# Two tiles of the first layer turned by VectorE instead of TensorE, the launch reordered, and a new order for everything else

## The chip, the cores and the metric

The kernel runs on one core of one Trainium2 chip. The metric is the device time of one execution, in microseconds (us); less is better. Before the change it is 876.21 us, the median of 3 runs (875.59 to 876.23).

TensorE (PE in the profile) multiplies a stationary 128x128 block with a moving block of up to 512 columns into a PSUM bank. VectorE (DVE) and ScalarE (ACT) read and write SBUF and PSUM, GpSimd (POOL) works in SBUF, and SyncE (SP) issues most of the DMAs. The program gives each engine its own list of instructions, and an instruction carries the waits for what it reads and overwrites.

## The reference: what is computed

Two layers over x of 2048 rows and 448 columns, in float32, each layer a linear attention block (A) and a dense block (B) with the same weights in both layers:

```
x = x + A(layernorm(x));  x = x + B(layernorm(x))       # twice
A: q, k, v = x @ wqkv in 16 heads of 28; phi(t) = (t + 1 if t > 0 else exp(t)) + 1e-6
   kv = sum over rows of phi(k) v;  z = sum over rows of phi(k)
   o = phi(q) kv / (phi(q) z + 1e-6);  A = o @ wo
B: gelu(x @ w1 + b1) @ w2 + b2                           # 448 -> 1792 -> 448
```

## The kernel before

The rows are cut into 16 tiles of 128 rows. To keep float32 accuracy, each operand is split into a rounded part (`hi`, type fp32r) and the rest (`lo`), and a product is made as hi*hi + hi*lo + lo*hi. That is why each product of a tile with a 448-column weight is a group of 11 matmuls of 448 columns.

In the attention stage of a layer each tile t is loaded (`ld`), its mean and variance are taken (`a`: three small VectorE instructions; the first tile's come first at the launch), GpSimd makes the reciprocal root (`ar`, tile `brs`), VectorE normalises it in place (`n`, the TENSOR_SCALAR x<-x,bmv,brs). The normalised tile has to be turned, columns onto partitions, before TensorE can multiply it. There are two ways:

- **by TensorE** (`T`, function `pe_turn`): ScalarE makes a doubled tail (`d`), four 128x128 transposes go into a PSUM bank `tp`, ScalarE casts the bank to the hi part `XH` (`xh`) and VectorE subtracts to get the lo part `XL` (`xl`, XL<-tp,XH).
- **in squares by VectorE** (`tu`, function `turn`): two STREAM_TRANSPOSE instructions turn 32x32 squares into the SBUF buffer `sq`, which two neighbouring tiles share; one DMA stores the pair to DRAM (`st`, sq_a<-sq), four DMAs read it back with the squares in their places (`sp`, sp<-sq_a), and `xh` and `xl` then read the SBUF buffer `sp` (XL<-sp,XH).

In layer 0, tiles 0 and 1 are turned by TensorE in halves at the launch (`ht`, `hx`, `hl`, `hk`), tiles 2 to 5 by `T`, tiles 6 to 15 in squares. In layer 1 all sixteen go in squares.

From the turned tile TensorE makes K (`K`, bank psk) and Q (`Q`, bank psq). phi of K goes ScalarE (`ke`), VectorE (`kp`), ScalarE (`kh`), VectorE (`kl`); VectorE adds phi(K) to a running sum (`za`). K has two PSUM banks, so tile t's K group can start only when `za` and `kl` of the K group two before it have read that bank. `G` adds up the normalised tile times phi(K) over the rows in four PSUM banks. After the sixteenth tile come the products with wv (`kv`, bank kvp), its masking to heads (`mask`), its hi part on ScalarE (`mkh`, kvh) and lo part on VectorE (`mkl`, kvl), and the products with wo (`m`). Then each tile's output (`o` for tiles 0 to 3, `oc` for the others), the second layernorm, and block B: `f` (11 matmuls of 512 columns), gelu (`g`), its split (`gh`, `gl`) and `y` (12 matmuls of 448 columns), for four groups of 14.

What sets the order is one string of tokens for each layer (`ORDER`), written out by a program that planned it beforehand. `run` calls each token's function in turn, and so each engine's list comes out in that order. `hot16` at the launch is 16 matmuls of 512 columns on a block of ones, which compute nothing. A token with > belongs to the next layer.

Of the kernel before, what the change touches and what calls it, by code (L numbers as in the profile page):

```python
# [118 lines left out]
def linear_attn_mlp_kernel(  # L119
# [84 lines left out]
    T = {}  # L204
# [141 lines left out]

    def stats(xs):
        st = small(6, "bst")  # L350
        dve.bn_stats(st, xs)  # L351
        mv = small(2, "bmv")
# [629 lines left out]
```

## Time and profile before

| what | before |
| --- | --- |
| median of 3 runs | 876.21 us (875.59 to 876.23) |
| the profiled execution's own time | 877.34 us |
| its span, first to last instruction | 875.6 us |
| TensorE busy | 870.3 us (99%), 4189 matmuls |
| VectorE busy | 477.5 us (55%) |
| ScalarE busy | 344.2 us (39%) |
| GpSimd busy | 208.7 us (24%) |
| granted TensorE clock | 1.0 |

Busy time of TensorE is the union of pipelined matmuls whose ends are modelled, so a short wait can hide in it. A row of the timeline holds start, length, engine, line, operation and tiles; waits of TensorE are best read from the starts of neighbouring rows. A line such as L365 is a line of the kernel before; in the changed kernel the same code stands 1 to 10 lines lower.

### The profile page before, as it was taken

What the parts mean: (1) busy time and instruction counts of PE and PEld (TensorE: products, weight loads), DVE (VectorE), ACT (ScalarE), POOL (GpSimd) and SP (SyncE); (2) the same over time, 40 slices, a digit from 0 to 9 for tenths busy, and PEclk for the clock granted to TensorE, in tenths of its full rate; (3) what the DMA queues carried; (4) which work ended last, traced back from release to release, by engine and by line L of the source; (5) the groups of instructions that cost most, each with busy time, mean ns of one, the idle gap of its engine ahead of it and who ended that gap; (6) DMA issues with size and microseconds to landing.
All of it is one profiled execution on the core that took longest, in us unless ns stands there. A gap on an engine that the chain in (4) does not pass through costs nothing.

```text
span 875.6 us, 11616 instructions
## 1 busy us (share of the span) xinstructions
PE 870.3 (99%) x4189; PEld 774.1 (88%) x4189; DVE 477.5 (55%) x974; ACT 344.2 (39%) x610; POOL 208.7 (24%) x247
## 2 busy tenths in 40 slices
PE   9999999999999999999999999999999999999998
PEld 7999998889888888888899999889898888888887
DVE  7887687758543534442379756875735616212112
ACT  6676744323223223322446555341332232223222
POOL 4555552543210020020022325240311110200000
PEclk9999999999999999999999999999999999999999
DMA  7666545543314203220347442363341251021101
GB/s 240 188 179 223 132 137 160 169 149 94 111 57 107 84 17 112 81 75 25 82 149 232 155 117 64 101 203 109 118 107 43 73 130 64 1 73 36 42 1 43
DMA packets 62762, 93.71 MB, mean 107 GB/s; under 512 B 8816, under 2 KB 57968, under 8 KB 62704
## 3 DMA queue, kind: packets, MB, share of 16 engines
q1 hardware_dynamic: 62400, 92.51, 35.1%
q8 instruction: 33, 0.54, 0.3%
q10 hardware_dynamic: 304, 0.46, 0.2%
q14 instruction: 25, 0.20, 0.1%
HBM read 55.65 MB, written 34.08 MB: 102 GB/s over the span
## 4 chain that ended last, share of the span: by engine, by line
PE 90%; issue 3%; DVE 2%; DMA 2%; ACT 1%; POOL 1%; SPq 0%; POOLq 0%; DVEq 0%; ACTq 0%
PE y L919 10%; PE y L918 10%; PE y L920 10%; PE hp L892 9%; PE hp L891 9%; PE hp L893 9%; PE hp L894 3%; PE hp L895 3%; PE psq L547 2%; PE psq L548 2%; PE psq L549 2%; PE op L827 2%; PE op L828 2%; PE op L826 2%; PE psk L547 1%
## 5 line engine op out<-in xcount | busy, mean ns | idle before, releaser
L910 DVE TENSOR_TENSOR gl<-g,gh 128x512 fp32r<-128x512 f32 x112 | 81.3, 729 | 265.1 <-ACT gh L215 265.1
L900 ACT ACTIVATE g<-hp,b1s 128x512 f32<-128x512 f32 x112 | 76.9, 688 | 258.1 <-PE hp L895 236.1
L919 PE MATMUL y<-w2l,gh 128*128 128x448 f32 x448 | 163.7, 365 | 0.0
L918 PE MATMUL y<-w2h,gh 128*128 128x448 f32 x448 | 163.6, 365 | 0.0
L920 PE MATMUL y<-w2h,gl 128*128 128x448 f32 x448 | 163.6, 365 | 0.0
L892 PE MATMUL hp<-XH,w1l 128*128 128x512 f32 x336 | 130.9, 390 | 0.0
L891 PE MATMUL hp<-XH,w1h 128*128 128x512 f32 x336 | 130.8, 389 | 0.0
L893 PE MATMUL hp<-XL,w1h 128*128 128x512 f32 x336 | 130.8, 389 | 0.0
L215 ACT CAST gh<-g 128x512 fp32r<-128x512 f32 x112 | 69.2, 621 | 137.8 <-PE y L919 131.7
L361 POOL TENSOR_TENSOR brs<-bve,mhalf 128x1 f32<-128x1 f32 x64 | 37.3, 586 | 358.7 <-DVE bve L355 325.5
L918 PEld LDWEIGHTS y<-w2h,gh 128*128 128x128 f32 x448 | 84.1, 188 | 7.4
L919 PEld LDWEIGHTS y<-w2l,gh 128*128 128x128 f32 x448 | 84.1, 188 | 7.3
L920 PEld LDWEIGHTS y<-w2h,gl 128*128 128x128 f32 x448 | 84.1, 188 | 6.6
L893 PEld LDWEIGHTS hp<-XL,w1h 128*128 128x128 f32 x336 | 63.1, 188 | 13.2
L891 PEld LDWEIGHTS hp<-XH,w1h 128*128 128x128 f32 x336 | 63.1, 188 | 12.6
L892 PEld LDWEIGHTS hp<-XH,w1l 128*128 128x128 f32 x336 | 63.1, 188 | 12.5
L757 POOL TENSOR_TENSOR pz<-pq,zb 128x448 f32<-128x448 f32 x32 | 37.3, 1170 | 50.0 <-DVE dn L762 37.1
L539 POOL TENSOR_TENSOR xnl<-x,xnh 128x384 fp32r<-128x384 f32 x32 | 32.6, 1017 | 58.4 <-ACT xnh L215 58.3
L351 DVE BATCH_NORM_STATS2 bst<-x 128x6 f32<-128x448 f32 x64 | 39.5, 617 | 7.7 <-DMA x<-in_A_x_dram 4.2
L894 PE MATMUL hp<-XH,w1x 128*128 128x512 f32 x112 | 43.6, 389 | 0.0
L895 PE MATMUL hp<-XL,w1x 128*128 128x512 f32 x112 | 43.6, 389 | 0.0
L855 POOL TENSOR_TENSOR x<-x,b2b 128x448 f32<-128x448 f32 x32 | 39.5, 1246 | 14.9 <-DVE xm L365 14.9
(174 smaller groups left out, 1569.2 us busy)
## 6 DMA issues: line engine op xcount, KB each, us to landing
x<-in_A_x_dram SPq DMA_DIRECT2D x32, 224.0 KB, 3.5
pq_d<-eq SPq DMA_DIRECT2D x32, 224.0 KB, 2.9
pq<-pq_d SPq DMA_DIRECT2D x32, 224.0 KB, 3.4
x<-x_d SPq DMA_DIRECT2D x32, 224.0 KB, 3.3
sq_a<-sq SPq DMA_DIRECT2D x13, 512.0 KB, 3.0
sp<-sq_a SPq DMA_DIRECT2D x52, 128.0 KB, 3.5
sq_q<-sq SPq DMA_DIRECT2D x12, 512.0 KB, 3.6
sp<-sq_q SPq DMA_DIRECT2D x48, 128.0 KB, 3.1
```

The costliest lines, as they stand in the source:

```text
L215: act.copy(out, src)
L351: dve.bn_stats(st, xs)
L891: pe.matmul(o, w1h[:, c, s], x.moving(x.hi, c), start=(c == 0), stop=False)
L892: pe.matmul(o, w1l[:, c, s], x.moving(x.hi, c), start=False, stop=False)
L893: pe.matmul(o, w1h[:, c, s], x.moving(x.lo, c), start=False, stop=False)
L894: pe.matmul(o, w1x[:, s], x.moving(x.hi, 3), start=False, stop=False)
L895: pe.matmul(o, w1x[:, s], x.moving(x.lo, 3), start=False, stop=True)
L900: act.activation(T[l, "g", n], T[l, "hp", n], AF.Gelu_apprx_tanh, bias=b1s[:, n % NF:n % NF + 1])
L910: dve.tensor_sub(lo, T[l, "g", n], f(hi))
L918: pe.matmul(o, gh[:, r], w2h[:, i, s], start=first, stop=False)
L919: pe.matmul(o, gh[:, r], w2l[:, i, s], start=False, stop=False)
L920: pe.matmul(o, gl[:, r], w2h[:, i, s], start=False, stop=last)
```

## The change

Layer 0 loses the tokens `T4`, `T5`, `d4`, `d5` (eight transposes and two tail copies) and gains `tu4`, `tu5`, `st2`, `sp2` (four STREAM_TRANSPOSE, one store, four reads). `hot16` becomes `hot15`. The statistics of tile 1 of layer 0 become two items, `as1` and `ag1`, which stand next to each other in the new string. In the launch's K product (`hk`) piece 1 of the weight is multiplied before piece 0. Both strings are otherwise the same tokens in another order, some of them moved across the border between the layers.

```diff
-        "ld0 a0 ar0 ld1 a1 n0 hot16 wkld0 wkld1:a wkld2 wkld3:a wkh1 wkl1 ht0 wkh0 ar1 wkl0 n1 d0 ht1 hx0 hl0 "
-        "hk0 wkh2 wkl2 wkh3 d1 ht3 hx1 hl1 wqld0 wqh0 ht2 hx2 wkl3:p hk1 hx3 hl2 hk2 hl3 wql0 hk3 ld2 wqld1 "
...
+        "ld0 a0 ar0 ld1 wkld0 wkld1:a wkld2 wkld3:a wqld0 ld2 wqld1 bld1:xn wqld2 wqld3 ld3 ld5 ld8 bld0:xn as1 "
+        "ag1 hot15 wkh1 ar1 n0 wkl1 d0 wkh0 ht0 n1 hx0 ht2 wkl0 d1 ht3 ld4 ht1 hl0 wkh2 wkl2 wkh3 hx1 hk0 hl1 "
...
-    def stats(xs):
-        st = small(6, "bst")
-        dve.bn_stats(st, xs)
+    def stats(xs, st=None):
+        if st is None:
+            st = small(6, "bst")
+            dve.bn_stats(st, xs)
...
+    def as_(l, t, e):
+        T["bs", l, t] = small(6, "bst")
+        dve.bn_stats(T["bs", l, t], T["x", l, t])
+
+    @op
+    def ag(l, t, e):
+        T["st", l, t] = stats(None, T["bs", l, t])
...
-            for c in range(2):
-                for w in range(2):
-                    pe.matmul(o, b.still(b.hi, t % 4, c), T[l, "w", "k", c][w], start=(c + w == 0), stop=False)
-            for c in range(2):
+            for c, w in ((1, 0), (1, 1), (0, 0), (0, 1)):
+                pe.matmul(o, b.still(b.hi, t % 4, c), T[l, "w", "k", c][w], start=(c == 1 and w == 0), stop=False)
+            for c in (1, 0):
                 pe.matmul(o, b.still(b.lo, t % 4, c), T[l, "w", "k", c][0], start=False, stop=False)
```

**TensorE at the launch.** First before, then changed (x_0 and x_1 are the normalised tiles 0 and 1, wk the pieces of K's weight).

```order
L232 MATMUL hot<-ones 128x512 x16
L469 MATMUL tp<-ident,x_0_103 128x128 x3
L469 MATMUL tp<-ident,tail 128x128
L493 MATMUL psk<-wk_153,XH 128x448
L493 MATMUL psk<-wk_154,XH 128x448
L493 MATMUL psk<-wk_146,XH 128x448
L493 MATMUL psk<-wk_147,XH 128x448
L495 MATMUL psk<-wk_153,XL 128x448
L495 MATMUL psk<-wk_146,XL 128x448
L469 MATMUL tp<-ident,x_1_113 128x128
```

```order
L232 MATMUL hot<-ones 128x512 x15
L479 MATMUL tp<-ident,x_0_103 128x128 x2
L479 MATMUL tp<-ident,x_1_113 128x128 x3
L479 MATMUL tp<-ident,tail 128x128
L479 MATMUL tp<-ident,x_0_103 128x128
L479 MATMUL tp<-ident,tail 128x128
L502 MATMUL psk<-wk_163,XH 128x448
L502 MATMUL psk<-wk_164,XH 128x448
L502 MATMUL psk<-wk_172,XH 128x448
L502 MATMUL psk<-wk_173,XH 128x448
```

All eight transposes of tiles 0 and 1 now stand ahead of the first product; before, the first product stood between them.

**VectorE where tiles 4 and 5 are turned.** Before there is no STREAM_TRANSPOSE for them; their place is this, before and changed.

```order
L365 TENSOR_SCALAR x_5_280<-x_5_280,bmv,brs 128x448
L351 BN_STATS bst<-x_4_294 128x6
L353 BN_AGGR bmv<-bst 128x2
L355 TENSOR_SCALAR bve<-bmv 128x1
L430 TENSOR_TENSOR XL<-tp,XH 128x512
L593 TENSOR_TENSOR za<-psk,za 128x448
L584 SCALAR_TENSOR_TENSOR kl<-psk,kh 128x448
```

```order
L366 TENSOR_SCALAR x_5_135<-x_5_135,bmv,brs 128x448
L403 STREAM_TRANSPOSE sq<-x_5_135 128x3x4x32
L404 STREAM_TRANSPOSE sq<-x_5_135 128x4x32
L366 TENSOR_SCALAR x_4_191<-x_4_191,bmv,brs 128x448
L571 SCALAR_TENSOR_TENSOR psk<-psk,ek 128x448
L403 STREAM_TRANSPOSE sq<-x_4_191 128x3x4x32
L404 STREAM_TRANSPOSE sq<-x_4_191 128x4x32
L571 SCALAR_TENSOR_TENSOR eq<-psq,eq 128x448
L602 TENSOR_TENSOR za<-psk,za 128x448
L593 SCALAR_TENSOR_TENSOR kl<-psk,kh 128x448
```

Four turning instructions have come in between the norms of tiles 5 and 4 and tile 1's `za` and `kl`.

**VectorE at the mask of layer 1**, before and changed.

```order
L686 TENSOR_TENSOR kvp<-kvp,mask 112x448
L770 SCALAR_TENSOR_TENSOR pq_1_5325<-pq_1_5325,rd 128x448
L770 SCALAR_TENSOR_TENSOR pq_0_5317<-pq_0_5317,rd 128x448
L696 TENSOR_TENSOR kvl<-kvp,kvh 112x448
L762 TENSOR_REDUCE dn<-pz 128x16
```

```order
L695 TENSOR_TENSOR kvp<-kvp,mask 112x448
L705 TENSOR_TENSOR kvl<-kvp,kvh 112x448
L779 SCALAR_TENSOR_TENSOR pq_0_5400<-pq_0_5400,rd 128x448
L771 TENSOR_REDUCE dn<-pz 128x16
L772 TENSOR_TENSOR dn<-dn,dc 128x16
```

The lo part `kvl` now follows the mask directly; the two scalings of Q stood between them.

More of the change, by code (lines that the diff above doesn't have):

```diff
@@ L445, in ar @@
     @op
+    def as_(l, t, e):
[4 more added lines that the diff above has]
+        T["st", l, t] = stats(None, T["bs", l, t])
+    @op
     def ar(l, t, e):
```

184 rows, old and new, of the table ORDER are left out of this document.

## The prediction

> **What bounds the kernel now.** I read the page's first two parts, then TensorE's timeline by the starts of neighbouring matmuls, because a busy share of 99% can hide short waits.
>
> ```profile
> PE 870.3 (99%) x4189; PEld 774.1 (88%) x4189; DVE 477.5 (55%) x974; ACT 344.2 (39%) x610; POOL 208.7 (24%) x247
> PE   9999999999999999999999999999999999999998
> DVE  7887687758543534442379756875735616212112
> ```
>
> TensorE is occupied from the first slice to the last, so time can be won in two ways only: TensorE gets less to do, or one of its few waits goes. It can be lost without bound, by new waits. VectorE is the next engine, and it is at 7 to 8 tenths exactly where tiles 4 and 5 are handled (slices of 21.9 us: the first seven are layer 0's attention stage). So I cost the work removed from TensorE, then each wait, then what the added VectorE work and DMAs may hold up.
>
> **Less work on TensorE: the transposes of tiles 4 and 5.**
>
> ```profile
> 27.84 0.36 PE L552 MATMUL psk<-wk,XL 128*128 128x448 f32 x1
> 28.04 0.49 PE L394 MATMUL tp<-ident,x 128*128 128x128 f32 x3
> 28.47 0.49 PE L394 MATMUL tp<-ident,x 128*128 128x128 f32 x3
> 28.83 0.45 PE L621 MATMUL G<-kh,xnh 128*128 128x448 f32 x1
> 29.11 0.37 PE L622 MATMUL G<-kl,xnh 128*128 128x448 f32 x1
> ```
>
> A 448-column matmul follows its neighbour after 0.20 us (27.84 to 28.04). The eight transposes take from 28.04 to 28.83, 0.79 us, and the matmul behind them needs 0.28 us to the next start instead of 0.20. Without them the row at 29.11 would start at 28.24: **-0.87 us**, and nothing hides it, since TensorE goes from one group to the next without a gap here.
>
> **The launch: one warm-up matmul fewer, another order.**
>
> ```profile
> 1.06 6.18 PE L232 MATMUL hot<-ones 128*128 128x512 f32 x16 [1.06 <-POOL ones L174]
> 7.07 0.49 PE L469 MATMUL tp<-ident,x 128*128 128x128 f32 x3
> 10.21 0.45 PE L497 MATMUL psk<-wk,XH 128*128 128x448 f32 x1
> 13.54 0.37 PE L547 MATMUL psq<-wq,XH 128*128 128x448 f32 x1
> 6.24 0.50 DVE L365 TENSOR_SCALAR x<-x,bmv,brs 128x448 f32<-128x448 f32 x1
> 8.11 0.51 DVE L365 TENSOR_SCALAR x<-x,bmv,brs 128x448 f32<-128x448 f32 x1
> 8.50 0.56 ACT L215 CAST sx<-stg 64x448 fp32r<-64x448 f32 x1
> 9.56 0.29 ACT L215 COPY tail<-x 128x128 f32<-128x128 f32 x1
> 9.20 1.29 POOL L300 TENSOR_TENSOR wk<-stg,sx 64x448 fp32r<-64x448 f32 x1 [2.05 <-ACT sx L215]
> ```
>
> Tile 0 is normalised at 6.74, its first transpose starts at 7.07 behind the last warm-up matmul. With one fewer it can start some 0.2 us earlier. But what follows is paced elsewhere. From 10.21 (second half of tile 0's product) TensorE runs at its own rate: 16 matmuls by 0.20 lead to 13.54. In the new order that second half still waits for its XH cast, which stands behind the same eight ScalarE instructions as before, so about 10.2 again. The norm at 8.11, tile 1's, now comes one place earlier, and its tail copy (9.56) goes ahead of the cast at 8.50, which moves by one copy, 0.3 at most, and with it GpSimd's 1.29 us piece, which the third matmul of that half needs. I bound the launch by -0.2 (the whole warm-up matmul) and +0.3 (the whole delay) and take **0**: what the earlier transposes win is spent waiting before 10.2. The split of tile 1's statistics changes nothing: VectorE's three instructions stand in the same place of its list. Swapping the weight pieces in the first product only lets the piece that arrives first go first; it lies ahead of 10.21 and is in the same bound.
>
> **Waits that may go.** Two are seen in the steady part.
>
> ```profile
> 542.04 0.61 DVE L686 TENSOR_TENSOR kvp<-kvp,mask 112x448 f32<-112x448 f32 x1
> 542.55 1.15 DVE L770 SCALAR_TENSOR_TENSOR pq<-pq,rd 128x448 f32<-128x448 f32 x2
> 542.68 0.53 ACT L215 CAST kvh<-kvp 112x448 fp32r<-112x448 f32 x1 [3.13 <-DVE kvp L686]
> 543.62 0.62 DVE L696 TENSOR_TENSOR kvl<-kvp,kvh 112x448 fp32r<-112x448 f32 x1
> 544.29 0.46 PE L716 MATMUL mp<-woh,kvl 112*112 112x448 f32 x1
> ```
>
> Layer 1's first product with wo would have issued its third matmul at 543.98 (0.20 behind the second) and does so at 544.29, because kvl comes after the two scalings of Q. In the new order kvl follows the mask: kvh is there at 543.2, kvl then runs to 543.9. **-0.31 us.**
>
> ```profile
> 73.24 1.15 POOL L343 TENSOR_TENSOR w1l<-stg,w1h 128x448 fp32r<-128x448 f32 x1
> 73.30 1.34 DVE L365 TENSOR_SCALAR x<-x,bmv,brs 128x448 f32<-128x448 f32 x1
> 75.36 0.59 DVE L593 TENSOR_TENSOR za<-psk,za 128x448 f32<-128x448 f32 x1
> 75.53 0.37 PE L552 MATMUL psq<-wq,XL 128*128 128x448 f32 x1
> 76.01 0.47 PE L547 MATMUL psk<-wk,XH 128*128 128x448 f32 x1
> ```
>
> A K group starts at 76.01 instead of 75.73, and its second matmul follows after 0.30 instead of 0.20: 0.38 us. It waited for `za` to leave its bank, and `za` was late because a norm took 1.34 us instead of 0.50, as long as GpSimd's operation beside it lasted. This meeting is an accident of the old order. The new one removes it but has accidents of its own; as the old order paid one such wait in 30 K groups, I let one new wait of the same size cancel it: **0**, bounded by -0.38 (none) and +0.4 (two).
>
> **The added work on VectorE.**
>
> ```profile
> L402 DVE STREAM_TRANSPOSE sq<-x 128x384 f32<-128x384 f32 x10 | 5.7, 570 | 0.1
> L403 DVE STREAM_TRANSPOSE sq<-x 128x128 f32<-128x128 f32 x10 | 2.7, 270 | 0.0
> L432 DVE TENSOR_TENSOR XL<-sp,XH 128x512 fp32r<-128x512 f32 x10 | 9.3, 938 | 0.0
> L430 DVE TENSOR_TENSOR XL<-tp,XH 128x512 fp32r<-128x512 f32 x8 | 5.3, 681 | 0.0
> 20.00:30.00 10.00, 10.00 (x57) 9.22 (x56) 9.69 (x25) 7.53 (x17) 5.77 (x9) 1.00 0.58 179
> 30.00:40.00 10.00, 10.00 (x51) 9.28 (x50) 7.65 (x21) 5.35 (x11) 6.14 (x8) 1.00 0.83 232
> L365 DVE TENSOR_SCALAR x<-x,bmv,brs 128x448 f32<-128x448 f32 x32 | 19.0, 598 | 9.3 <-POOL brs L361 9.1
> ```
>
> Each turn is 0.57 + 0.27 us, two are 1.7. Each XL now reads two SBUF buffers instead of a bank and a buffer: 938 against 681 ns, 0.5 for two. VectorE gets 2.2 us more, ScalarE loses two tail copies. In 20 to 30 us VectorE has 0.3 us free, in the next ten 2.3 (the rows' third busy column is VectorE's): the work fits only by sliding into the second stretch. What is queued behind the turns is tile 1's `za` and `kl`, which G1 reads. K1 is done at 13.5 us in both orders, G1 now starts near 25.7 (13.54, five groups of 11 by 2.23, two turns with 1.0), so there is room, and I cost it at **0**; uncovered it would be +2.2.
>
> The Trainium skill, page "SBUF — State Buffer", section "Who interferes with whom", says that a VectorE instruction with two SBUF inputs contends with a GpSimd instruction that reads SBUF, and that the later one blocks. The 938 against 681 ns agree, and so does the norm at 73.30. By that rule the change trades transposes which nobody can block for XL work that GpSimd can; were those 0.5 us on the path, the sum would be -0.7 instead of -1.2.
>
> **The new chain for tile 4.**
>
> ```profile
> 22.13 0.50 DVE L365 TENSOR_SCALAR x<-x,bmv,brs 128x448 f32<-128x448 f32 x1
> 452.87 0.32 SPq L408 DMA_DIRECT2D sq_a<-sq  x1
> 455.85 1.74 SPq L414 DMA_DIRECT2D sp<-sq_a  x4
> 461.47 0.62 ACT L215 CAST XH<-sp 128x512 fp32r<-128x512 f32 x1
> 65.56 0.46 SPq L408 DMA_DIRECT2D sq_a<-sq  x1
> 17.87 0.33 SPq L609 DMA_DIRECT2D pq_d<-eq  x1
> 69.24 0.57 ACT L215 CAST w2h<-stg 128x448 fp32r<-128x448 f32 x1 [0.50 <-DMA stg<-in_B_w_dram]
> 70.51 1.75 SPq L414 DMA_DIRECT2D sp<-sq_a  x4
> 76.26 1.14 ACT L215 CAST XH<-sp 128x512 fp32r<-128x512 f32 x2 [2.20 <-DMA sp<-sq_a]
> ```
>
> The norm of tile 5 was VectorE's 38th row at 22.13 and is the 38th again. Behind it stand two turns, a norm and a phi: 2 x 0.77 (they overlap a little) + 0.43 + 0.54 = 2.5, so the store can go at 24.7. A quick chain is 8.6 us from store to XH (452.87 to 461.47), a slow one 10.7 (65.56 to 76.26, where XH had waited 2.20 for it). XH is then there at 33.3 + 0.6 = 33.9, XL at 34.6. K4 comes on TensorE behind nine groups of 11 (Q0, Q1, G0, Q2, K2, G1, K3, Q3, G2) and two turns, 9 x 2.23 + 1.0 from 13.54: 34.6, its first XL matmul 0.4 later. So the quick chain just makes it: **0**. On SyncE the store stands behind the first Q store, which went at 17.87 before, and a load. Behind the five new DMAs wait the second Q store and weights of block B. Their casts stand in ScalarE's list and can hold it up, by 0.5 us in the row at 69.24; ScalarE is free for half of this stretch (5.35 of 10), so I charge nothing.
>
> **Sum**: -0.87 + 0 - 0.31 + 0 + 0 + 0 = -1.18 us. The profiled execution, 877.34, would be 876.16; it is 1.13 above the median, and 876.21 - 1.18 = **875.0**.
>
> **Rivals.**
>
> - Everything clean: no new waits at all, the launch gives its 0.2. -0.87 - 0.31 - 0.38 - 0.2 = -1.76: 874.45 or a little less. For it: both waits it removes come from orders that the change undoes. Against: the 32 norms of the attention stages take 598 ns in the mean instead of 500, so one in eight or so meets GpSimd, and a new order has its own.
> - Tile 4's squares come late (slower). With the slow chain XH is 2.1 us later, 36.0 against 34.6, XL 36.7 against 35.0: TensorE stands 1.4 to 1.7. -1.18 + 1.7 = +0.5: 876.7. It decides from a chain over 9.3 us. For it: DMA is busiest in this stretch (0.83 in 30 to 40, rows above). Against: layer 1 of the old kernel ran such a chain quickly.
> - VectorE sets the pace of layer 0's attention stage: its 2.2 us come onto TensorE's path through banks freed late by `za` and `kl`. -1.18 + 2.2 = +1.0: 877.2, and 878 to 879 if three to five late norms add 0.38 each. For it: 9.69 of 10 in the stretch. Against: a K bank is mostly used again only three groups of 11 (6.7 us) later. The rule cited above would make this one likelier.
>
> **How the numbers follow.** Likeliest, near -1.2: 0.46, own range 874.5 to 875.7. Clean: 0.24. Late squares: 0.14. VectorE's pace: 0.16. About 0.2% (1.75 us) is what a measurement here can tell from no change. Faster by more than that, below 874.46: the greater part of the clean case and a little of the likeliest, 0.25. Slower by more, above 877.96: most of the last case and a little of the late squares, 0.15. The rest, 0.60, is the same. The range leaves out the far end of the clean case and the upper half of the last: 873.9 to 877.5.
>
> **What would show it.** Right: TensorE's G group follows the K and Q groups at 0.20 us steps with no transposes of tiles 4 and 5; Q0 starts at 13.4 to 13.6; the L725 matmul of layer 1's first product with wo comes 0.2 behind its neighbour; waits of 0.3 to 0.4 in layer 0's attention stage number one or so. Wrong: K4's first matmul (L556, near 34.6) starts with a gap after G2 (late squares); several K groups start late behind `za` (VectorE's pace); or gaps stand in layer 1 or block B, where I looked at no new wait.

## The result, and the profile after

The changed kernel takes **881.41 us** (median of six executions, 878.66 to 882.25) against 876.00 of the kernel before beside it (875.59 to 876.23): a ratio of **1.0056, interval 1.0045 to 1.0066**. (The ratio and its interval are worked out from the single executions; the quotient of the two medians would be 1.0062.) It is slower; 875.0 us was predicted, with a range of 873.9 to 877.5.

The profiled execution took 881.94 us with a span of 880.2 (before: 877.34 and 875.6). The table sets the starts of the first matmul of each stage against each other; the last column is what the stage before that row lost or won.

| first matmul of | before, us | after, us | later by | of it new |
| --- | --- | --- | --- | --- |
| Q0, layer 0 | 13.54 | 13.44 | -0.09 | -0.09 |
| z, layer 0 | 102.86 | 103.52 | +0.66 | +0.75 |
| first o, layer 0 | 119.03 | 120.98 | +1.96 | +1.30 |
| K0, layer 1 | 440.68 | 442.52 | +1.84 | -0.12 |
| z, layer 1 | 535.57 | 536.14 | +0.57 | -1.27 |
| product with wv, layer 1 | 538.20 | 538.77 | +0.57 | 0.00 |
| first product with wo, layer 1 | 543.57 | 546.57 | +3.00 | **+2.43** |
| first o, layer 1 | 549.54 | 554.08 | +4.54 | **+1.54** |
| first f, layer 1 | 569.04 | 573.14 | +4.09 | -0.45 |
| end of the span | 875.61 | 880.22 | +4.61 | +0.52 |

Two of these need a word first. In the long stretches of K, Q and G groups TensorE issues a 448-column matmul either every 202.7 ns or every 206.7 ns for the whole stretch, and one order of instructions showed both (last section). The +0.75 and the -1.27 are that: the profile after had the longer step in layer 0 from 26 to 103 us, the profile before had it in layer 1 from 471 to 536. It comes to 1.3 to 1.5 us each and cancels here.

The page after shows nothing of the loss in its first two parts:

```profile
PE 871.6 (99%) x4180; PEld 774.1 (88%) x4180; DVE 486.0 (55%) x978; ACT 343.7 (39%) x608; POOL 212.1 (24%) x247
PE   9999999999999999999999998999999999999998
```

One digit, the 25th (528 to 550 us), has fallen from 9 to 8. TensorE's waits name it. First the start of the list of the kernel after (engine, line, whom it waited for: us in total, times, longest; two waits of 0.2 follow), then the whole list of the kernel before:

```profile
PE mp L723 <- ACT kvh L215: 2.3, 1, 2.3
PE hot L232 <- POOL ones L174: 1.1, 1, 1.1
PE tp L479 <- DVE x L366: 0.8, 2, 0.5
```

```profile
PE hot L232 <- POOL ones L174: 1.1, 1, 1.1
PE tp L469 <- ACT tail L215: 0.2, 1, 0.2
```

The wait is for kvh, the hi part of the masked product with wv in layer 1. Its releaser is ScalarE, but ScalarE had itself been idle for 4.48 us, waiting for the mask. The timeline of the kernel after goes back to the cause:

```profile
540.65 2.26 POOL L717 TENSOR_TENSOR wol<-wot,woh 112x448 fp32r<-112x448 f32 x2 [0.83 <-ACT woh L215]
541.25 0.61 DVE L771 TENSOR_REDUCE dn<-pz 128x16 f32<-128x448 f32 x1
541.90 3.25 DVE L772 TENSOR_TENSOR dn<-dn,dc 128x16 f32<-128x16 f32 x1
542.87 1.16 POOL L766 TENSOR_TENSOR pz<-pq,zb 128x448 f32<-128x448 f32 x1
543.96 0.36 PE L561 MATMUL psq<-wq,XL 128*128 128x448 f32 x1
543.98 2.22 POOL L717 TENSOR_TENSOR wol<-wot,woh 112x448 fp32r<-112x448 f32 x2
545.18 0.25 DVE L774 RECIPROCAL rd<-dn 128x16 f32<-128x16 f32 x1
545.35 0.61 DVE L695 TENSOR_TENSOR kvp<-kvp,mask 112x448 f32<-112x448 f32 x1
545.99 0.53 ACT L215 CAST kvh<-kvp 112x448 fp32r<-112x448 f32 x1 [4.48 <-DVE kvp L695]
546.57 0.45 PE L723 MATMUL mp<-woh,kvh 112*112 112x448 f32 x1 [2.26 <-ACT kvh L215]
```

Third row: an addition of 16 columns (`pd` of tile 0: denominator plus constant) takes 3.25 us. The same line took this, over its 32 instances in the kernel after (minimum, median, maximum in ns):

```profile
L772 DVE TENSOR_TENSOR dn<-dn,dc x32: 174/176/3246, 107.2 to 704.7; 128x16 f32<-128x16 f32 x32
```

It starts while GpSimd works on wol, and GpSimd's next two instructions follow without a pause; the addition ends where GpSimd passes from the first wol of the last pair to the second (543.98 plus half of 2.22 is 545.09). The mask stands behind it in VectorE's list, although the product it masks was complete at 542.1. So TensorE stands from 544.2 to 546.6.

What follows the wait is slow as well. TensorE's clock in three windows of 3.41 us of the kernel after (columns: PE busy, PEld, VectorE, ScalarE, GpSimd, then the granted clock, DMA share, GB/s):

```profile
540.85:544.26 3.41, 3.41 (x24) 2.96 (x22) 3.38 (x3) 0.66 (x2) 3.41 (x4) 1.00 0.00 0
544.26:547.67 3.41, 1.15 (x5) 0.68 (x5) 2.78 (x5) 0.53 (x1) 3.03 (x3) 1.00 0.00 0
547.67:551.08 3.41, 3.41 (x15) 2.99 (x14) 3.14 (x8) 1.65 (x3) 0.00 (x0) 0.50 0.14 49
```

In the third the clock is 0.50. That is the +1.54 of the table: 2.43 + 1.54 = 3.97 of the 4.61 us.

The next largest loss is layer 0's +1.30 between z and o. Both kernels have the same 102 matmuls there, and TensorE's starts show three waits: 0.30 between the two matmuls of z, 0.33 for a copy of G in the product with wv, and 0.38 for `ql` of an earlier tile in the turning of Q. That is 1.01; 0.11 more is the step from z to the Q group behind it (0.31 instead of 0.20), and 0.18 is not traced. A further wait of 0.32 lies just ahead of z and so belongs to the row before.

### The profile page after: what moved, and what is told of

It reads as the page before. It is cut to its first block, busy times and chain, and to the rows that moved or that the text cites. A ratio compares the mean times of both kernels' runs of the same rounds, so it can differ in the third digit from the quotient of the medians.

```text
span 880.2 us, 11628 instructions
## 1 busy us (share of the span) xinstructions
PE 871.6 (99%) x4180; PEld 774.1 (88%) x4180; DVE 486.0 (55%) x978; ACT 343.7 (39%) x608; POOL 212.1 (24%) x247
## 4 chain that ended last, share of the span: by engine, by line
PE 85%; DVE 2%; issue 1%; POOL 0%; DMA 0%; ACT 0%; DVEq 0%; POOLq 0%
PE y L929 10%; PE y L928 10%; PE y L927 10%; PE hp L901 9%; PE hp L900 9%; PE hp L902 9%; PE hp L903 3%; PE hp L904 3%; PE op L836 2%; PE op L835 2%; PE op L837 2%; PE psq L556 1%; PE psq L557 1%; PE psq L558 1%; PE psk L558 1%; PE psk L557 1%
## 5 line engine op out<-in xcount | busy, mean ns | idle before, releaser
L362 POOL TENSOR_TENSOR brs<-bve,mhalf 128x1 f32<-128x1 f32 x64 | 40.6, 638 | 334.8 <-DVE bve L356 334.6
L548 POOL TENSOR_TENSOR xnl<-x,xnh 128x384 fp32r<-128x384 f32 x32 | 33.9, 1061 | 58.9 <-ACT xnh L215 53.8
L433 DVE TENSOR_TENSOR XL<-sp,XH 128x512 fp32r<-128x512 f32 x52 | 38.2, 743 | 9.6 <-ACT XH L215 9.5
```

What stands on the lines that cost most here:

```text
L362: pool.tensor_tensor(rs, ve, mhalf, op=OP.pow)
```

## The experiments

All ratios are to the kernel before, timed beside the run on the same chip; its medians there were 876.16, 877.4, 876.49 and 876.17 us. The string diffs show the tokens around the edit.

**1. The small addition behind the mask.** In layer 1 `pd0` is moved, nothing else.

```diff
- ol2 kv Q11 pd0 oh3 ol3 oh1 pl2 mask mkh mkl pz2 m2
+ ol2 kv Q11 oh3 ol3 oh1 pl2 mask mkh mkl pd0 pz2 m2
```

> The changed kernel with one token of layer 1 moved: the denominators of tile 0 (pd0) come behind the mask and its lo part on VectorE instead of ahead of them. Theory 1: TensorE stood 2.4 us at 543.96 only because the 16-column addition in pd0 was held for 3.25 us behind GpSimd's operations and the mask stood behind it. Then the first product with wo starts about 0.2 us behind Q11, the half clock after the wait is gone too, and the time falls by 2.4 to 4 us to 877 to 879. Rival: kvp or kvh is late for a reason of its own (the mask would be held by GpSimd as well, or TensorE's product kv ends late); then the wait stays and the time stays near 881.

Measured: 878.36 us (877.85 to 879.14, ten executions), **1.0024, 1.0015 to 1.0033**. The product with wo follows that with wv after 5.39 us (after: 7.80; before: 5.37), the clock stays at 1.0. From 1.0056 the ratio falls by 0.0032, 2.8 us. The addition of the same tile is now short, as GpSimd happens to be idle:

```profile
542.80 0.17 DVE L772 TENSOR_TENSOR dn<-dn,dc 128x16 f32<-128x16 f32 x1
542.85 1.15 POOL L766 TENSOR_TENSOR pz<-pq,zb 128x448 f32<-128x448 f32 x1 [1.67 <-DVE dn L771]
543.30 1.17 DVE L779 SCALAR_TENSOR_TENSOR pq<-pq,rd 128x448 f32<-128x448 f32 x1
543.95 2.63 POOL L717 TENSOR_TENSOR wol<-wot,woh 112x448 fp32r<-112x448 f32 x2
```

But the stage isn't healed: the scaling of Q is now held (1.17 instead of 0.62 us), tile 0's turning waits 0.47 for it, and the last two products with wo wait 0.37 and 0.41 for wol. First product with wo to first o takes 6.93 us, against 5.97 before.

**2. The addition left out.** The order as changed; one instruction less.

```diff
-        dve.tensor_tensor(dn, dn, T[l, "dc"], op=OP.add)
+        if (l, t) != (1, 0): dve.tensor_tensor(dn, dn, T[l, "dc"], op=OP.add)
```

> The changed kernel in its own order, with one VectorE instruction left out: tile 0 of layer 1 no longer adds the constant term dc to its denominator (the addition of 128x16 that took 3.25 us at 541.90 us in the changed kernel), so that tile's output is without that 1e-6 term. Theory (this addition, which reads two SBUF operands, is held while GpSimd works through its three neighbouring instructions, and the mask, kvh and the first product with wo wait behind it): kvp to first product comes down from 7.80 us to 5.4 to 5.7, no half clock follows, and the time is 877.5 to 878.7. Rival (the wait is that of the mask or of something else that the order brought, and the addition only shows it): the next two-input instruction takes the 3 us over, the wait of TensorE stays at 2 us or more and the time at 880.5 to 882.

Measured: 878.05 us (876.72 to 880.05, ten executions), **1.0011, 1.0001 to 1.0020**. Product with wv to product with wo 5.39 us, no half clock. The mask, which stood 3.5 us behind the end of that reduction in the kernel after, now follows directly:

```profile
541.77 0.61 DVE L771 TENSOR_REDUCE dn<-pz 128x16 f32<-128x448 f32 x1
542.41 0.25 DVE L774 RECIPROCAL rd<-dn 128x16 f32<-128x16 f32 x1
542.64 0.63 DVE L695 TENSOR_TENSOR kvp<-kvp,mask 112x448 f32<-112x448 f32 x1
```

So 16 columns of work cost about 4 us of the kernel. The reduction, the reciprocal and the mask are not held here, although GpSimd runs beside them: the first two have one SBUF input each, and the mask reads a PSUM bank beside one. One SBUF input alone is no protection, though: the norm at 73.30 in the prediction reads one tile and two single columns and took 1.34 us instead of 0.50. The rival, that the next instruction takes TensorE's wait over, is out; the next one with two SBUF inputs, a scaling of Q, is held for 1.73 us, but it stands behind the mask and kvl.

**3. The wait kept, TensorE kept busy in it.** Ten matmuls on the block of ones stand in the wait.

```diff
- ol2 kv Q11 pd0 oh3
+ ol2 kv Q11 hot10 pd0 oh3
```

> The changed kernel with ten matmuls on ones (which compute nothing) put between Q11 and the first product with wo in layer 1, where TensorE stands for 2.4 us. Theory 2: the granted clock falls to 0.5 for 3.4 us because of this stand-still, and costs about 1.5 us more behind it. Then the first product starts where it did, no record of 0.5 is left inside the span, and the time falls by 1 to 1.7 us. Rival: the clock falls for another reason; then the time is the same or up to 0.3 us longer and the 0.5 stays.

Measured: 879.85 us (878.83 to 880.88, four executions), **1.0038, 1.0023 to 1.0053**. The addition again takes 3.27 us and the first product with wo comes as late as in the kernel after (7.82 us behind the product with wv), but first product with wo to first o takes 5.89 us instead of 7.51:

```profile
544.40:547.80 3.40, 3.40 (x16) 2.39 (x14) 2.77 (x4) 0.53 (x1) 3.40 (x4) 1.00 0.00 0
547.80:551.20 3.40, 3.40 (x21) 2.91 (x21) 3.33 (x9) 2.20 (x5) 0.26 (x1) 1.00 0.00 0
```

The half clock is a consequence of the wait, and costs 1.6 us.

**4. and 5. The lone filler matmul `fl`.** My third theory was that the place of `fl` sets the step of 203 or 207 ns, since the kernel before has it early in layer 0, behind G0, and the kernel after ahead of z. First in layer 0 of the changed kernel, then in layer 0 of the kernel before:

```diff
- G14 ke15 za14 fl blo15
+ ar6 xl3 bld3:xn fl K3
```

> The changed kernel with the single warm-up matmul of layer 0 (fl) moved from ahead of z to ahead of K3, just behind the G group from which the matmuls follow one another every 0.207 us instead of 0.203. Theory 3: a 512-column matmul in between brings TensorE back to the quicker step, which then holds to z: 370 matmuls by 0.004, 1.5 us less in layer 0's attention stage, time near 880. Rival: the step is set by what else runs there (DMA, VectorE, the buffers); then 0.207 stays and the time stays.

```diff
- xl2 ke1 a7 fl ar7
+ zh zl sh15 fl z
```

> The kernel before with only this token moved: fl from behind G0 to ahead of z in layer 0, as in the change. Theory 3: if fl is what kept layer 0 at the 0.203 us step, the step becomes 0.207 from a group of turns on and the time rises by up to 1.5 us, to 877.5. Rival: the step depends on which groups of turns and products follow each other, and the four transposes in a row of tiles 4 and 5 kept it quick; then the time stays within 0.3 us of 876.0.

Measured: 881.56 us (880.48 to 883.07, four executions), **1.0059, 1.0043 to 1.0074**, no different from the changed kernel; and 877.82 us (876.12 to 878.76, ten), **1.0015, 1.0005 to 1.0025**. The profile of the first has the short step in layer 0, that of the second too from 30 us on and in layer 1 as well. But the run with only `pd0` moved has the same order as the changed kernel in layer 0, and its profile has the short step there:

```profile
30.00:100.00 70.00, 70.00 (x340) 63.57 (x340) 51.51 (x109) 47.41 (x90) 37.54 (x46) 1.00 0.68 208
```

```profile
30.00:100.00 70.00, 70.00 (x348) 64.86 (x347) 52.60 (x110) 48.36 (x92) 37.78 (x46) 1.00 0.69 210
```

(First the kernel after, then the run with `pd0` moved: 340 and 348 matmuls in the same 70 us.) One order, both steps: the theory falls. The kernel before came out 1.3 us slower with `fl` moved (0.4 to 2.2 by the interval), and no profile shows why: in this run's, Q0 starts 0.52 later than in the profile before, but that lies ahead of the token that was moved.

**6. The attention sums in the old order.** In both layers the tokens from `zh` to `Q15` are put into the relative order of the kernel before; all else is as changed.

> The changed kernel, launch, squares and all else as changed, but in both layers the instructions from the running sum's end (zh) to the fourth Q group after it stand in the order in which the kernel before had them. Theory (the loss lies in that stage alone: 2.4 us of wait and 1.5 us of half clock in layer 1, about 0.8 us of short waits in layer 0): 875.4 to 876.6, first product with wo to first o in layer 1 back from 7.51 to about 6.0 us, kvp to first product from 7.80 to 5.4. Rival (the rest of the new order loses as well, in layer 0's tiles, layer 1 or block B): 877.3 to 879.

Measured: 884.43 us (881.52 to 885.15, four executions), **1.0080, 1.0061 to 1.0098**: neither theory. In layer 1 first product with wo to first o is 5.74 us as I expected, but the old order of this stage does not fit the new order around it:

```profile
PE tp L395 <- DVE xm L366: 2.2, 1, 2.2
```

Layer 0's second layernorm is now late, and so are the copies of G in both layers (waits of 1.0 and 0.4 us). It shows nothing on where the changed kernel loses; it shows how tightly these lists lock into each other.

**7. and 8. Squares alone.** The kernel before with tiles 4 and 5 in squares, first with the four reads directly behind their store and G2 ahead of K4, then with loads moved ahead of the reads and G3 ahead of K4 too.

```diff
- n7 ar4 qe2 n4 d4 K2 ke2 sh2 bld0:xn bhi0 ... K3 ... T4 T5
+ n7 ar4 qe2 n4 tu4 st2 sp2 K2 ke2 sh2 bld0:xn bhi0 ... K3 ...
```

> The kernel before with one part of the change alone: tiles 4 and 5 of layer 0 turned in squares by VectorE, with G of tile 2 ahead of K of tile 4 so that the squares' trip through DRAM has its time; launch and all else as before. Theory (eight transposes of TensorE, 0.87 us by the prediction, fall out of a chain that nothing else delays): 0.5 to 1.1 us under the kernel before of the same chip, 875.1 to 875.7. Rival (VectorE or the trip through DRAM sets the pace instead): 0 to 1 us over it.

```diff
+ a7 bld0:xn fl ... n4 tu4 st2 K2 ... G1 ke3 sh3 ar9 sl3 n9 kp3 kh3 kl3 ld13 ld8 sp2 xh4 xh5 Q3 G2 G3 a8 xl4 xl5 blo3 K4
```

> The kernel before with tiles 4 and 5 of layer 0 turned in squares, as in the run that put the four reads of the squares right behind their store, but with the loads that others wait for (a weight of block B, tiles 13 and 8) ahead of those reads on the DMA queue, and with G of tiles 2 and 3 ahead of K of tile 4. Theory (the squares themselves cost TensorE nothing, and what the other run lost, 8.2 us of ScalarE waiting for a weight, was the queue held behind the store): no wait over 0.5 us of TensorE between 25 and 45 us, and 0.9980 to 0.9995 times the kernel before. Rival (the squares of these two tiles are too late for K of tile 4 at this place in any order): a wait of 1 us or more before K of tile 4, and 1.0005 times or more.

Measured: 884.84 us (883.54 to 885.88), **1.0090, 1.0074 to 1.0106**, and 882.28 us (881.36 to 883.84), **1.0067, 1.0054 to 1.0079**. The first lies far above what theory and rival gave; in the second the rival was right. The timeline of the first shows how the queue does it:

```profile
27.94 0.33 SPq L408 DMA_DIRECT2D sq_a<-sq  x1
30.88 1.76 SPq L414 DMA_DIRECT2D sp<-sq_a  x4
32.73 0.38 SPq L250 DMA_DIRECT2D stg<-in_B_w_dram  x1
35.97 0.56 ACT L215 CAST w1h<-stg 128x448 fp32r<-128x448 f32 x1 [8.17 <-DMA stg<-in_B_w_dram]
```

The reads are issued 2.9 us behind the store whose data they need, and what stands behind them in SyncE's list waits with them: the weight is issued at 32.73, and its cast holds up ScalarE for 8.17 us, with `kh` of tile 2 behind it: TensorE stood 4.8 us for that `kh`. In the second, ScalarE's hold-up is gone, but the DMAs are full while the squares are under way (a share of 1.0 from 31.8 to 38.7 us), and the squares come late:

```profile
31.79 1.80 SPq L414 DMA_DIRECT2D sp<-sq_a  x4
39.95 1.14 ACT L215 CAST XH<-sp 128x512 fp32r<-128x512 f32 x2 [4.66 <-DMA sp<-sq_a]
```

K4 waits 2.49 us. In the changed kernel the store goes at 23.97, XH is made at 31.56, and K4 comes at 34.78 without a gap. So the squares don't come free by themselves: in the kernel before, in the better of the two orders tried, they cost 5.8 us. Two things differ in the changed kernel: its launch loads weights of block B and tiles 3, 5 and 8 early, and its norm of tile 4 starts at 22.26 us instead of about 26.6 in the first of these runs. That these make the squares free is likely, but no run shows it. The prediction's "late squares" is a real mechanism, only not in the changed kernel.

**9. The kvl wait alone.** The kernel before, layer 1 only.

```diff
- mask pm1 mkh pm0 mkl pz2 ... m3 pT0 qh0 ql0 qp11 pT1 m0
+ mask pm1 mkh mkl pm0 pz2 ... m3 pT1 pT0 qh0 ql0 qp11 m0
```

> The kernel before with one part of the new order alone: in layer 1 kvl stands right behind the mask, pm of tile 0 behind kvl, and tile 1 is turned ahead of tile 0. Theory (the 0.31 us wait for kvl in the kernel before goes, as the prediction had it): 0.15 to 0.45 us under the kernel before, 875.6 to 876.0. Rival (the wait only moves to the turning of tile 0 or to wol): within 0.15 us of it or over it.

Measured: 877.18 us (875.87 to 878.12, eleven executions), **1.0002, 0.9993 to 1.0011**: the same. In its trace the third matmul of the product with wo follows after 0.20 us, so the wait of 0.31 is gone, and 0.24 stands a microsecond later:

```profile
544.74 0.37 PE L715 MATMUL mp<-wol,kvh 112*112 112x448 f32 x1
544.94 0.41 PE L716 MATMUL mp<-woh,kvl 112*112 112x448 f32 x1
545.98 0.44 PE L714 MATMUL mp<-woh,kvh 112*112 112x448 f32 x1
546.42 0.46 PE L715 MATMUL mp<-wol,kvh 112*112 112x448 f32 x1
```

From product with wv to first o the stage takes 11.24 us against 11.34. The term of -0.31 was worth -0.11 where it was tried, as the rival had it: TensorE only reached the next late tile, wol, sooner.

**10. and 11. The named waits out by order.** The changed kernel with `pd0` as in run 1 and, in layer 0, `pm1` behind the last copy of G and tile 2's turning behind the last product with wo. In layer 1 run 10 puts wol of the groups 0 and 1 ahead of pz of tile 2, run 11 only the first of them (the first and the second line with a +).

```diff
- mkl pd0 pz2 m2 ... ol0 qp10 pm2 ol1 ... pT0 m0 mh0 m1 ml0 qh0
+ mkl pd0 ol0 ol1 pz2 m2 ... qp10 pm2 ... m0 mh0 m1 ml0 pT0 qh0
+ mkl pd0 ol0 pz2 m2 ... qp10 pm2 ol1 ... m0 pT0 mh0 m1 ml0 qh0
```

> The changed kernel with five of its short waits taken out by order alone: in layer 1 pd of tile 0 behind kvl, wol of groups 0 and 1 ahead of pz of tile 2 and tile 0 turned behind the products with wo; in layer 0 the copy of the last G bank ahead of pm of tile 1 and tile 2 turned behind the last product with wo. Theory (the loss of the changed kernel is the sum of the named waits and the half clock): against the run with only pd moved (1.0024 times the kernel before) the waits of 0.47, 0.37 and 0.41 us in layer 1 and of 0.31 and 0.37 us in layer 0 go, 1.9 us or 0.22%, so 0.999 to 1.001 times the kernel before. Rival (the waits only move on to the next thing that is late on VectorE or GpSimd): 1.0015 times or more, with waits of the same sum in the trace.

> The changed kernel with pd of tile 0 behind kvl in layer 1, only the first wol of the pair 0 and 1 ahead of pz of tile 2 (so that GpSimd is idle when the small addition of pd runs), the first of the last two products with wo ahead of tile 0's turning, and layer 0's two moves as in the run before. Theory (the loss is the named waits, and an addition that starts while GpSimd is idle isn't held): the addition takes under 0.5 us, first product with wo to first o in layer 1 5.9 to 6.3 us (6.93 with only pd moved), 0.9990 to 1.0008 times the kernel before. Rival (the order of this stage can't be had without a wait of a microsecond): 1.002 times or more.

Measured, run 10: 880.52 us (878.88 to 881.22, five executions), **1.0045, 1.0031 to 1.0059**. The rival was right, and more plainly than it said. GpSimd has four wol in a row and then two pz, and the addition of 16 columns runs into them once more:

```profile
538.87 4.59 POOL L717 TENSOR_TENSOR wol<-wot,woh 112x448 fp32r<-112x448 f32 x4 [0.83 <-ACT woh L215]
542.75 2.96 DVE L772 TENSOR_TENSOR dn<-dn,dc 128x16 f32<-128x16 f32 x1
543.43 2.25 POOL L766 TENSOR_TENSOR pz<-pq,zb 128x448 f32<-128x448 f32 x2
```

It ends at 545.71, when GpSimd's run ends (545.68). TensorE stands 1.49 us for tile 0's turning and 1.53 for a Q bank that VectorE frees late.

Run 11: 877.82 us (876.58 to 880.34, twelve executions), **1.0019, 1.0010 to 1.0027**. The addition takes 0.18 us, as expected, with GpSimd idle for 0.44 us ahead of its pz. But first product with wo to first o is 6.77 us, not 5.9 to 6.3: 0.27 for wol, and 0.82 for the Q bank. So the theory's time, 1.0008 at most, was missed. In layer 0 both runs have 16.7 us from z to first o (17.17 in run 1, 16.17 before): those two moves did what was expected, and one wait of 0.46 within z is left. I found no order of layer 1's stage in the new surroundings as good as the old one in the old.

**12. The transposes back.** Run 11 with tiles 4 and 5 turned by TensorE, behind K3.

```diff
- n4 kp1 bhi0 blo0 sh3 sl3 tu4 st2 sp2 kh1 ... qe2 ke2 ... K3 kp2
+ n4 kp1 bhi0 blo0 sh3 sl3 kh1 ... qe2 d5 d4 ke2 ... K3 T4 T5 kp2
```

> The same kernel with one part of the change undone: tiles 4 and 5 of layer 0 turned by TensorE again (eight transposes and two tail copies, behind K of tile 3) instead of in squares. Theory (the squares of the change cost TensorE nothing and the transposes 0.87 us by the prediction): first Q to z in layer 0 0.7 to 1.1 us longer than in the run with the squares, as long as both have the same step of the 448-column matmuls; the time 0.0005 to 0.0015 higher in the ratio. Rival (VectorE, freed of 2.2 us, or the queue, freed of a store and four reads, gives the time back): less than 0.4 us longer.

Measured: 883.86 us (882.96 to 885.07, five executions), **1.0084, 1.0071 to 1.0097**. It tells nothing on the 0.87 us: the second turning needs a bank that VectorE leaves only after XL of tile 4, TensorE stands 3.45 us for it, and half a clock follows (33.83 to 40.65 us). An undo of one part in a list planned around it is no undo. What the term was worth is read from the stage instead, below.

## Why the prediction was wrong, and where it was right

**Less work on TensorE: right as far as a sum can show it.** Between Q0 and z no gap over 0.12 us is left in the profile after. With the short step in both, that stage takes 89.32 us in the kernel before and 88.59 in the run with `pd0` moved, whose layer 0 is that of the changed kernel: -0.73. The prediction's terms were -0.87 for the transposes and -0.38 for the `za` wait that goes; the new wait of 0.32 just ahead of z is the one "of the same size" that I let cancel it. -0.87 - 0.38 + 0.32 = -0.93, so 0.2 us is missing. No run shows the -0.87 by itself.

**VectorE, tile 4's chain: right.** The lines of the kernel after:

```profile
23.97 0.33 SPq L409 DMA_DIRECT2D sq_a<-sq  x1
31.56 0.60 ACT L215 CAST XH<-sp 128x512 fp32r<-128x512 f32 x1
34.78 0.37 PE L556 MATMUL psk<-wk,XH 128*128 128x448 f32 x1
```

The store went at 23.97 (24.7 worked out), XH was there at 32.16 (33.9), K4 started at 34.78, directly behind G2 (34.6). One reading in the working was off: the norm of tile 5 is the 40th VectorE row of the trace before, not the 38th, and the 38th of the trace after, where it started at 21.02 instead of 22.13; so the chain began 1.1 us earlier than the prediction had it. VectorE's 2.2 us set no pace. The rivals "late squares" and "VectorE's pace" did not come about.

**The launch: right in the profile after, wrong in others.** Q0 started at 13.44, inside the 13.4 to 13.6 given. But in four of the nine profiles of kernels with the new launch, Q0's eighth matmul waits 0.83 to 0.90 us; in none of the five with the old. The bound of +0.3 left this out. The kernel after, then run 11, around the lo part of a weight of Q:

```profile
14.24 0.63 DVE L298 TENSOR_TENSOR wq<-stg,wq 128x448 fp32r<-128x448 f32 x1
14.28 1.46 POOL L548 TENSOR_TENSOR xnl<-x,xnh 128x384 fp32r<-128x384 f32 x1 [0.97 <-ACT xnh L215]
```

```profile
14.13 1.02 POOL L548 TENSOR_TENSOR xnl<-x,xnh 128x384 fp32r<-128x384 f32 x1 [0.85 <-ACT xnh L215]
14.21 1.41 DVE L298 TENSOR_TENSOR wq<-stg,wq 128x448 fp32r<-128x448 f32 x1
```

Whoever starts first keeps its time and the other is stretched, VectorE from 0.63 to 1.41 or GpSimd from 1.02 to 1.46. The two starts lie 0.04 and 0.08 us apart: a race that each execution decides anew.

**Waits that may go: the step that failed.** The prediction said: "In the new order kvl follows the mask: kvh is there at 543.2, kvl then runs to 543.9. -0.31 us." It looked at what stands between the mask and kvl, and not at what the new order put *ahead* of the mask. There stand the three instructions of `pd0`, one of them with two SBUF inputs, and beside them GpSimd has five instructions almost without a pause. In place of -0.31 came +2.43, and behind it +1.54, most or all of it from the half clock (1.6 by run 3). The sign that was named for it did not come either: the third matmul (L725) starts at 547.23, 0.37 behind the second and not 0.2, because the mask, kvh and kvl are all late now. Where the term was tried alone it was -0.11 (run 9).

**"One new wait of the same size": wrong in size and in number.** That estimate took the one late norm of the old trace as the measure, 0.38 us, and bounded the sum by two of them. The old trace held a better one, which I didn't look for. The line of the small addition in the kernel before, and the product with wv beside it:

```profile
538.20 3.31 PE L681 MATMUL kvp<-gt,wvt 128*112 128x112 f32 x32
539.28 1.46 DVE L763 TENSOR_TENSOR dn<-dn,dc 128x16 f32<-128x16 f32 x1
544.80 1.29 DVE L763 TENSOR_TENSOR dn<-dn,dc 128x16 f32<-128x16 f32 x1
```

1.46 and 1.29 us for what usually takes 0.17: held by GpSimd's wol and pz, as in the kernel after. It was nearly harmless there, since TensorE still had Q11 to do behind the product with wv. But not quite: VectorE had no pause from the first of them to the mask, which started at 542.04 although its product was complete at 541.5. Without the hold kvl could have come half a microsecond earlier, which is more than the wait of 0.31, so that wait was not due to the two scalings alone. With those two rows the question would have been what the new order puts behind an addition of 1.3 us or more. The prediction quoted the rule from the Trainium skill, page "SBUF — State Buffer", section "Who interferes with whom", for the XL work and the norms, where it turned out to cost nothing; it bore on the smallest two-input instruction in the list. The runs agree with the rule on what is held (for how long, see the last section), and the race at the launch agrees with that section's sentence "Issue order, not op shape, decides who blocks." The norm at 73.30, which the prediction counted for the rule, is no case of two SBUF tiles.

**The wrong stage.** Both terms with a doubt were placed in layer 0, where the tokens change; the text named gaps in layer 1 "where I looked at no new wait" as what would make it wrong, and gave them no chance of their own. 3.97 of the 4.61 us came from there. In layer 0 the loss of 1.30 lies in the attention sums, where the prediction had no term either.

**Sum.** Predicted -1.18. Measured in the profiles, with the 203 and 207 ns stretches taken out of both (+1.5 in layer 0, -1.27 in layer 1): -0.09 launch, -0.75 from Q0 to z, +1.30 layer 0's sums, -0.12 block B of layer 0, +2.43 and +1.54 in layer 1, -0.45 and +0.52 to the end: +4.4 us. The last two and the 0.2 us missing above are too small and too spread to say what they are.

## What to carry to other kernels

When a change reorders whole lists, the terms that can be worked out are the small ones: here those that a run could tell came within 0.2 us, and a wait that nobody had costed was, with its half clock, over three times as large as their sum. So go through the new order for what stands directly *ahead* of each item that TensorE waits for, on every engine, and price a VectorE instruction with two SBUF inputs there by the unbroken run of GpSimd beside it, not by its median (0.18); even its longest row in the old trace (1.46 us) was less than half of the 3.25 that it took. And a wait of TensorE over 2 us can cost 1.6 us more through the clock, if most of it falls into one window (below): ten useless matmuls in it took that back.

## What the runs showed of the hardware

**A held VectorE instruction may not get in between two of GpSimd's.** The addition of 16 columns waited through two borders between GpSimd instructions in the kernel after (542.87 and 543.98) and through two in run 10 (543.43 and the one between its two pz), and got in at the third or at the end: 3.25 (3.27 in run 3) and 2.96 us. So the price isn't one GpSimd instruction's time, but up to that of the whole unbroken run beside it. That GpSimd is what holds it, all fourteen traces show together. They have 447 of these additions. The 311 that start while no GpSimd instruction runs take 0.18 us at most. All 133 that take over 0.2 us start beside one, and end 0.03 to 0.08 us behind the end of one. Of the 45 over 0.9 us, 26 got in at the first end of a GpSimd instruction (up to 1.14 us), 15 at the second (1.29 to 1.83) and 4 at the third (2.96 to 3.27); what decides at which stays open.

**The clock is set in windows of 3.41 us, by how busy TensorE was in the one before.** All stretches of half clock inside the kernels are 3.41 or 6.83 us long, and the full clock ahead of the one in the kernel after lasted 542.72 us, 159 times 3.413. Cut at those borders, the window ahead of the half clock had TensorE busy for 1.15 us (kernel after, shown above) and 1.44 us (the second run with squares alone):

```profile
38.70:42.11 3.41, 1.44 (x6) 1.01 (x7) 1.52 (x4) 1.14 (x2) 0.00 (x0) 1.00 0.84 303
42.11:45.52 3.41, 3.41 (x11) 3.02 (x10) 2.16 (x7) 1.97 (x4) 2.20 (x3) 0.50 0.70 176
```

In run 6 a wait of 2.33 us fell across a border, TensorE was busy for 1.84 of the first window and 2.72 of the second, and the clock stayed at 1.00:

```profile
135.36:138.77 3.41, 1.84 (x11) 1.45 (x10) 1.81 (x4) 2.48 (x5) 2.45 (x3) 1.00 0.08 15
138.77:142.19 3.42, 2.72 (x14) 2.35 (x15) 3.02 (x6) 0.59 (x1) 0.29 (x1) 1.00 0.52 186
```

So what counts is not the wait's length but how much of it falls into one window; the bound lies between 1.46 (run 12's window, half clock behind it) and 1.84 us busy of 3.41. Cut that way, the five windows of all fourteen traces with 1.46 us or less at full clock are followed by half clock, and no other window inside the kernels is. Once at half, the clock needs more: in run 12 a window at half clock with 2.07 us busy was followed by another at half. The Trainium skill, page "TensorE: Matmul & The Clock Gate", section "What's actually happening", gives a free-running window of 3413 ns, and the rows agree with that; for falling back it names an idle window, and here 1.15 to 1.46 us of work in the window did not prevent it. That one of the six executions of the changed kernel took 878.66 us and the others 880.93 or more would fit a wait cut in two by a border; only one of them was profiled, so this is not shown.

**Two steps of TensorE.** Stretches of K, Q and G groups run at 202.7 or 206.7 ns from matmul to matmul, 1.3 to 1.5 us apart over a stretch. The longer step set in between 21 and 27 us in layer 0 (at 41 in run 12) and at about 471 us in layer 1, and where it lasted it ended with z. The executions of the kernel before fall into two groups (875.6 to 876.9 and 877.1 to 877.8 us) that lie about as far apart. What decides it stays open; the order doesn't, since one order had both.
